# Linear-attention products in quarters of the array, two units at a time, in a kernel that ends in a SiLU network

## The chip, the cores and the metric

The kernel runs on one core of a Trainium2 chip. Its metric is the device time of one execution in microseconds, taken as the median of several runs. TensorE is written PE below, VectorE DVE, ScalarE ACT, GpSimd POOL and the engine that issues most transfers SP.

## The reference

The inputs are r, k and v of shape 4 x 8 x 768 x 48 (batch, heads, time, head dimension), decays w and bonuses u of 8 x 48, and the two weight matrices of a network, 384 x 2048 and 2048 x 384. The first part walks through time with a 48 x 48 state per batch and head:

```
for t in range(S):
    cur = einsum('bhd,bhe->bhde', u * k[t], v[t])
    y[t] = einsum('bhd,bhde->bhe', r[t], state + cur)
    state = w * state + einsum('bhd,bhe->bhde', k[t], v[t])
```

The second part takes y as 3072 tokens of 384 values, multiplies by w_in, applies h * sigmoid(h), and multiplies by w_out. The result is 3072 x 384 in float32.

## The kernel before, in words

Time is cut into 6 chunks of 128 steps (C = 128, HC = 64 is half of it). A **unit** is one chunk of one batch: 24 units, numbered so that unit i is batch i % 4 of chunk i // 4. Four units make up one chunk, which is called a stage here (units 4 to 7, 8 to 11 and so on); its 512 tokens go through the network together.

In a unit the recurrence becomes matrix products. `turn` transposes r and k with PE (16 fp32 transposes of 64 rows, two row halves of the array) into a PSUM tile `t`; `decay` multiplies them by powers of w on DVE, giving `rT` and `kT`. `product` (L202) multiplies kT with rT for each of 8 heads, keys on partitions and queries along the free axis, in fp32, with contraction 48: heads in partitions 0 to 47 and 64 to 111 use the upper and the lower rows of the array. `masked` zeroes the pairs whose key is not earlier than the query. `outputs` (L216) adds state times r (L223) and masked product times v (L228) in the PSUM tile `ys`, and forms the state's increment from keys and values (L235). `evict_y` (L245) adds the bonus term and writes `y16`; `state` updates the state; `turn_y` (L274) transposes y16 into `xT`, by PE and a copy on ACT for units 0 to 5, by a DMA transpose on SP for units 6 to 23.

The network is `l1` (three fp16 matmuls of 512 columns and a SiLU on ACT for each of 16 column blocks; it reads `xT` of all four units of the stage) and `l2` (four fp16 matmuls of 384 columns; four such parts make one output tile, which is copied and stored). These calls are **fillers** in one first-in first-out list; `fill(n)` emits the next n of them, or fewer where the list is empty. In stages from the second on, 32 fillers come in with each finished stage (16 of l1, 16 of l2) and 8 are emitted per unit.

The order of instructions on each engine is the order of the Python text: nothing reorders it. The work of units 0 to 3 is written out by hand with part of the first stage's l1. Then a loop over single units follows; each iteration calls, in order: product(i), the POOL work of unit i+1, masked(i), fill(2), turn(i+1), decay(i+1), outputs(i), evict_y(i), turn_y(i), state(i), load(i+4), casts of i+1, fill(6), and after the last unit of a stage the list gets the fillers of that stage. When the loop starts the list holds 24 fillers: 8 of l1 (each two column blocks of half the stage) and 16 of l2.

[...]Tiles tagged `att` (t, a, ys) take two banks each and have two buffers; tiles tagged `moe` (l1's hps, l2's ops, yT) take one bank each and have four.

Of the kernel before, what the change touches and what calls it, by code (L numbers as in the profile page):

```python
# [8 lines left out]
FP = mybir.dt.float32  # L9
F16 = mybir.dt.float16  # L10
# [5 lines left out]
def kernel(  # L16
# [14 lines left out]
    C = 128  # L31
# [18 lines left out]
    def unit(i):  # L50
        return divmod(i, B)

    wpT = cst.tile([PR, NP], FP)
    w_bc = cst.tile([128, HD], FP)
    u_bc = cst.tile([128, H, D], FP)
    rin = [big.tile([128, H, 64], FP, name=f"rin{i}") for i in range(NIN)]
    kin = [big.tile([128, H, 64], FP, name=f"kin{i}") for i in range(NIN)]
    vin = [big.tile([128, H, D], FP, name=f"vin{i}") for i in range(NIN)]
    kc = [big.tile([128, H, 64], F16, name=f"kc{i}") for i in range(2)]
    st = [big.tile([PR, NP, PW], FP, name=f"st{b}") for b in range(B)]  # L60
    st16 = [big.tile([PR, NP, PW], F16, name=f"stb{b}") for b in range(B)]
    win = big.tile([128, NQ, DFF], F16)
# [8 lines left out]
    def load(i):  # L71
        if i >= NU:
            return
        ld(i, rin, r)
        ld(i, kin, k)
        ld(i, vin, v)
# [21 lines left out]
    for i in range(NIN):  # L98
# [12 lines left out]
    nc.gpsimd.affine_select(  # L111
        out=maskM, in_=maskM, compare_op=ALU.is_ge, fill=0.0,
        base=-1, channel_multiplier=-1, pattern=[[1, C]])
    ident16 = cst.tile([128, 128], F16)
    nc.gpsimd.tensor_copy(out=ident16, in_=ident)
    for b in range(B):
# [3 lines left out]
    for i in range(NIN):  # L120
        nc.vector.memset(rin[i][:, :, D:64], 0.0)
        nc.vector.memset(kin[i][:, :, D:64], 0.0)
    for i in range(2):
        nc.vector.memset(kc[i][:, :, D:64], 0.0)

    lnwT = cst.tile([PR, NP], FP)
# [22 lines left out]
    def L(i):  # L149
        return live.setdefault(i, {})  # L150

    def bonus_products(i):
        n = i % NIN
        ku = wrk.tile([128, H, D], FP, name="ku")
        nc.gpsimd.tensor_tensor(out=ku, in0=kin[n][:, :, 0:D], in1=u_bc, op=ALU.mult)  # L155
        L(i)["rku_f"] = wrk.tile([128, H, D], FP, name="rku_f")
        nc.gpsimd.tensor_tensor(out=L(i)["rku_f"], in0=rin[n][:, :, 0:D], in1=ku, op=ALU.mult)  # L157

    def decayed_k(i):
        eng = nc.vector if i < B else nc.gpsimd  # L160
        eng.tensor_tensor(out=kc[i % 2][:, :, 0:D], in0=kin[i % NIN][:, :, 0:D],  # L161
                                in1=lamC, op=ALU.mult)

    def bonus_sum(i):
        L(i)["rku"] = wrk.tile([128, H], FP, name="rku")
        nc.vector.tensor_reduce(out=L(i)["rku"], in_=L(i)["rku_f"],  # L166
                                axis=mybir.AxisListType.X, op=ALU.add)

    def bonus_v(i):
# [2 lines left out]
                                in1=L(i)["rku"].unsqueeze(2).broadcast_to([128, H, D]),  # L172
                                op=ALU.mult)

    def cast_v(i):
        L(i)["v16"] = wrk.tile([128, H, D], F16, name="v16", bufs=3)
        nc.scalar.copy(out=L(i)["v16"], in_=vin[i % NIN])

    def turn(i):
        n = i % NIN  # L180
        t = L(i)["t"] = ps.tile([128, 2, 2, NP, HC], FP, name="t", tag="att", bufs=2)
        for x, src in enumerate((rin, kin)):
            flat = src[n].rearrange("p h d -> p (h d)")
            for p in range(NP):
                for y in range(2):
                    rows = slice(HC * y, HC * y + HC)
                    nc.tensor.transpose(t[0:PR, y, x, p, :], flat[rows, 128 * p:128 * p + PR],  # L187
                                        ident[rows, rows])

    def decay(i):  # L190
        for x, key, lam in ((0, "rT", lamR), (1, "kT", lamK)):
            L(i)[key] = wrk.tile([PR, NP, C], FP, name=key)
            nc.vector.tensor_tensor(  # L193
                out=L(i)[key].rearrange("p g (y t) -> p y g t", y=2),
                in0=L(i)["t"][0:PR, :, x], in1=lam.rearrange("p g (y t) -> p y g t", y=2),
                op=ALU.mult)

    def cast_r(i):
        L(i)["rT16"] = wrk.tile([PR, NP, C], F16, name="rT16")
        nc.scalar.copy(out=L(i)["rT16"], in_=L(i)["rT"])  # L200

    def product(i):  # L202
        a = L(i)["a"] = ps.tile([128, 2, NP, C], FP, name="a", tag="att", bufs=2)
        rT, kT = L(i)["rT"], L(i)["kT"]
        for p in range(NP):
            for j, r0 in ((0, 0), (1, 64)):
                nc.tensor.matmul(a[:, j, p, :], kT[r0:r0 + D, p, :], rT[r0:r0 + D, p, :],  # L207
                                 start=True, stop=True)

    def masked(i):  # L210
        am = L(i)["am"] = wrk.tile([128, 2, NP, C], F16, name="am")
        nc.vector.tensor_tensor(  # L212
            out=am.rearrange("p h g c -> p (h g) c"), in0=L(i)["a"].rearrange("p h g c -> p (h g) c"),
            in1=maskM.unsqueeze(1).broadcast_to([128, H, C]), op=ALU.mult)

    def outputs(i):  # L216
        sc, b = unit(i)
        v16 = L(i)["v16"]
        ys = L(i)["ys"] = ps.tile([128, 2, 512], FP, name="ys", tag="att", bufs=2)
        y = ys[:, 0, 0:HD].rearrange("p (h d) -> p h d", h=H)  # L220
        for p in range(NP):
            if sc:
                nc.tensor.matmul(y[:, 2 * p:2 * p + 2, :],  # L223
                                 L(i)["rT16"][0:PR, p, :],
                                 st16[b][:, p, :], start=True, stop=False)
            for j in range(2):
                h = 2 * p + j
                nc.tensor.matmul(y[:, h, :], L(i)["am"][:, j, p, :], v16[:, h, :],  # L228
                                 start=not sc, stop=(not sc or j == 1))
        if sc < NCH - 1:  # L230
            sps = ys[:, 1, 0:HD].rearrange("p (g n) -> p g n", g=NP)
            kf = kc[i % 2].rearrange("p h d -> p (h d)")
            vf = v16.rearrange("p h d -> p (h d)")
            for p in range(NP):
                nc.tensor.matmul(sps[:, p, :], kf[:, 128 * p:128 * p + 128],  # L235
                                 vf[:, PW * p:PW * p + PW], start=True, stop=True)
# [6 lines left out]
                                    in1=wCT.unsqueeze(2).broadcast_to([PR, NP, PW]), op=ALU.mult)  # L243

    def evict_y(i):  # L245
        y = L(i)["ys"][:, 0, 0:HD].rearrange("p (h d) -> p h d", h=H)
        L(i)["y16"] = wrk.tile([128, H, D], F16, name="y16")
        nc.vector.tensor_tensor(out=L(i)["y16"], in0=y, in1=L(i)["vu"], op=ALU.add)  # L248

    def state(i):  # L250
        sc, b = unit(i)
        if sc == NCH - 1:
            return
        sps = L(i)["ys"][:, 1, 0:HD].rearrange("p (g n) -> p g n", g=NP)
        for p0, c0 in ((0, 0), (64, D)):
            dst = st[b][p0:p0 + D, :, c0:c0 + D]
            src = sps[p0:p0 + D, :, c0:c0 + D]
            if sc:
                nc.vector.tensor_tensor(out=dst, in0=src,  # L259
                                        in1=L(i)["sdec"][p0:p0 + D, :, c0:c0 + D], op=ALU.add)  # L260
            else:
                nc.scalar.copy(out=st16[b][p0:p0 + D, :, c0:c0 + D], in_=src)
                nc.scalar.copy(out=dst, in_=src)
        if sc:
            nc.gpsimd.tensor_copy(out=st16[b], in_=st[b])  # L265
# [22 lines left out]
    def l1(sc, b0, nb, ft):  # L288
        if sc not in gts:
            gts[sc] = wrk.tile([128, NFT, B * C], F16, name="gT", bufs=2)  # L290
        m = B // nb
        hps = ps.tile([128, m, nb * C], FP, name="hps", tag="moe", bufs=4)
        for f in range(m):
            for q in range(NQ):
                nc.tensor.matmul(hps[:, f, :], win[:, q, (ft + f) * 128:(ft + f + 1) * 128],  # L295
                                 xts[sc][:, q, b0:b0 + nb, :].rearrange("p b t -> p (b t)"),
                                 start=(q == 0), stop=(q == NQ - 1))
        nc.scalar.activation(out=gts[sc][:, ft:ft + m, b0 * C:(b0 + nb) * C], in_=hps, func=AF.Silu)  # L298
# [21 lines left out]
    def fill(n):  # L320
        for _ in range(n):
            if fillers:
                fillers.pop(0)()
# [87 lines left out]
    bonus_sum(4)  # L411
    bonus_v(4)
    decayed_state(4)
    fillers.extend([lambda ft=ft: l1(0, 2, 2, ft) for ft in range(0, NFT, 2)])
    fillers.extend(second(0))

    for i in range(B, NU):
        sc, b = unit(i)
        product(i)
        if i + 1 < NU:  # L420
            bonus_products(i + 1)
            decayed_k(i + 1)
        masked(i)
        fill(2)
        if i + 1 < NU:
            turn(i + 1)
            decay(i + 1)
        outputs(i)
        evict_y(i)
        turn_y(i, i < 6)  # L430
        state(i)
        load(i + NIN)
        if i + 1 < NU:
            cast_v(i + 1)
            cast_r(i + 1)
            bonus_sum(i + 1)
            bonus_v(i + 1)
            decayed_state(i + 1)
        fill(6)
        if b == B - 1:  # L440
            fillers.extend(first(sc) + second(sc))
    fill(len(fillers))


# [28 lines left out]
```

## Time and profile before

| what | value |
|---|---|
| median of 3 runs | 214.6 us (214.12 to 215.39) |
| the profiled execution | 214.33 us, of which the span is 212.6 us |
| PE busy | 192.9 us, 91% of the span |
| DVE, ACT, POOL busy | 103.0, 99.0, 118.1 us |
| l1 matmuls (L295) | 68.2 us busy, 336 records |
| l2 matmuls (L307) | 65.9 us busy, 384 records |
| products (L207) | 30.6 us busy, 384 records for 192 instructions |
| transposes of r and k (L187) | 11.6 and 10.6 us busy, 192 records each |
| DMA transposes of y16 (L279) | 18, 2.3 us in the median from issue to landing |

The span runs from the first to the last instruction of the profile. "Busy" is time in which at least one instruction of the group is in flight. Matmuls overlap, so that a mean duration (304 ns for a record of L207) is longer than the step from one record to the next. A line of the timeline gives start, length and kind of a run of like instructions, and in brackets the idle time ahead of it and what ended it.

### The profile page before, as it was taken

The page shows a single profiled execution, that of the slowest core. Times are in us where ns is not written, and L with a number is a line of the kernel's source. Part 1 is how long each engine was busy: PE and PEld are TensorE (multiplying, and loading weights), DVE is VectorE, ACT ScalarE, POOL GpSimd, SP SyncE. Part 2 cuts the span into 40 slices and gives each one's busy share as a digit, 9 for nine tenths or more (in the row PEclk, how much of TensorE's full clock was granted, in tenths as well). Part 3 has the DMA queues.
Part 4 walks back from the last instruction along what each step waited for, and adds up shares of the span by engine and source line. Part 5 has one row for each costly group of instructions (what it writes and reads, how often), then busy time and mean ns, then how long its engine had stood idle before and what let it go on. Part 6 is the DMA issues. An engine that isn't in the chain of part 4 may idle for free.

```text
span 212.6 us, 4734 instructions
## 1 busy us (share of the span) xinstructions
PE 192.9 (91%) x1858; PEld 122.7 (58%) x1858; DVE 103.0 (48%) x173; ACT 99.0 (47%) x190; POOL 118.1 (56%) x151
## 2 busy tenths in 40 slices
PE   1677898798986999999999999999999999999993
PEld 0566587665663655675556666556665556654551
DVE  3677386543656545563573474565456246300121
ACT  2403868633321767233864324783226782159400
POOL 8677549966296567558558557756854662000000
PEclk9999999999998899999999999999999999999999
DMA  6899999999175255277346267525627010220011
GB/s 113 177 180 212 206 203 172 195 159 211 40 167 130 58 113 102 52 185 156 93 87 130 59 167 189 100 48 114 138 89 187 19 22 18 78 94 0 0 74 74
DMA packets 90262, 24.49 MB, mean 115 GB/s; under 512 B 83328, under 2 KB 90240, under 8 KB 90240
## 3 DMA queue, kind: packets, MB, share of 16 engines
q1 hardware_dynamic: 85824, 20.65, 44.6%
q0 software_dynamic: 3712, 3.15, 9.6%
q10 hardware_dynamic: 704, 0.40, 0.9%
q8 instruction: 14, 0.23, 0.4%
q14 instruction: 8, 0.07, 0.1%
HBM read 20.84 MB, written 4.72 MB: 120 GB/s over the span
## 4 chain that ended last, share of the span: by engine, by line
PE 86%; DVE 5%; DMA 3%; issue 2%; POOL 1%; ACT 0%; ACTq 0%; DVEq 0%; POOLq 0%
PE hps L295 31%; PE ops L307 30%; PE a L207 12%; PE t L187 7%; DMA u_bc<-in_u_dram 2%; PE ys L223 2%; PE ys L228 2%; DVE rT L193 2%; PE ys L235 1%; DMA xT<-y 1%; DVE y L248 1%; PE yT L283 1%; DVE am L212 1%; DVE kT L193 1%; DVE kc L161 1%
## 5 line engine op out<-in xcount | busy, mean ns | idle before, releaser
L295 PE MATMUL hps<-xT,win 128*128 128x512 f16 (+1 forms) x336 | 68.2, 357 | 2.1 <-DMA xT<-y 1.6
L307 PE MATMUL ops<-wout,gT 128*128 128x384 f16 x384 | 65.9, 326 | 0.0
L298 ACT ACTIVATE gT<-hps 128x512 f16<-128x512 f32 x96 | 56.1, 597 | 17.7 <-PE hps L295 14.5
L212 DVE TENSOR_TENSOR am<-a,maskM 128x1024 f16<-128x1024 f32 x24 | 29.4, 1224 | 56.1 <-PE a L207 56.0
L307 PEld LDWEIGHTS <-gT 128*128 128x128 f16 x384 | 36.2, 98 | 23.6
L295 PEld LDWEIGHTS <-win 128*128 128x128 f16 x336 | 32.3, 100 | 29.7 <-issue 2.5
L207 PE MATMUL a<-rT,kT 48*128 48x128 f32 x384 | 30.6, 304 | 3.4 <-DVE kT L193 3.4
L207 PEld LDWEIGHTS a<-rT,kT 48*128 48x128 f32 x384 | 25.8, 204 | 10.8 <-issue 6.5
L265 POOL CAST stb<-st 112x384 f16<-112x384 f32 x16 | 8.1, 505 | 39.1 <-DVE st L259 26.2
L171 POOL TENSOR_TENSOR vu<-vin,rku 128x384 f32<-128x384 f32 x24 | 19.9, 830 | 17.5 <-DVE rku L166 17.1
L193 DVE TENSOR_TENSOR rT<-t,lamR 112x512 f32<-112x512 f32 x24 | 16.5, 689 | 20.6 <-PE t L187 14.7
L200 ACT CAST rT<-rT 112x512 f16<-112x512 f32 x20 | 12.4, 618 | 29.2 <-DVE rT L193 29.2
L155 POOL TENSOR_TENSOR ku<-kin,u_bc 128x384 f32<-128x384 f32 x24 | 24.1, 1003 | 3.0 <-DMA u_bc<-in_u_dram 1.8
L157 POOL TENSOR_TENSOR rku_f<-rin,ku 128x384 f32<-128x384 f32 x24 | 24.6, 1025 | 1.9
L312 ACT COPY osb<-ops 128x384 f32<-128x384 f32 x20 | 9.6, 480 | 29.3 <-PE ops L307 29.3
L161 POOL TENSOR_TENSOR kc<-kin,lamC 128x384 f16<-128x384 f32 x20 | 20.0, 1001 | 0.0
L193 DVE TENSOR_TENSOR kT<-t,lamK 112x512 f32<-112x512 f32 x24 | 16.3, 680 | 0.0
L187 PE MATMUL t<-ident,rin 64*112 64x64 f32 x192 | 11.6, 247 | 5.1 <-DMA rin<-in_r_dram 4.2
L187 PEld LDWEIGHTS t<-ident,rin 64*112 64x112 f32 x192 | 8.2, 145 | 13.1 <-DVE am L212 4.6
L166 DVE TENSOR_REDUCE rku<-rku_f 128x8 f32<-128x384 f32 x24 | 13.2, 550 | 2.3 <-POOL rku_f L157 1.7
L248 DVE TENSOR_TENSOR y<-ys,vu 128x384 f16<-128x384 f32 x24 | 13.2, 548 | 1.8 <-PE ys L235 1.1
L242 POOL TENSOR_TENSOR sdec<-st,wCT 112x384 f32<-112x384 f32 x16 | 13.2, 828 | 0.0
(46 smaller groups left out, 132.2 us busy)
## 6 DMA issues: line engine op xcount, KB each, us to landing
rin<-in_r_dram SPq DMA_DIRECT2D x24, 192.0 KB, 3.0
kin<-in_k_dram SPq DMA_DIRECT2D x24, 192.0 KB, 3.5
vin<-in_v_dram SPq DMA_DIRECT2D x24, 192.0 KB, 3.6
out_dram<-osb SPq DMA_DIRECT2D x24, 192.0 KB, 2.5
win<-in_moe_w_in_dram POOLq DMA_DIRECT2D x4, 384.0 KB, 6.1
wout<-in_moe_w_out_dram POOLq DMA_DIRECT2D x4, 384.0 KB, 8.6
xT<-y SPq DMA_TRANSPOSE x18, 2.3
u_bc<-in_u_dram ACTq DMA_DIRECT2D x1, 192.0 KB, 5.0
```

The lines of the kernel that those rows point to most:

```text
L155: nc.gpsimd.tensor_tensor(out=ku, in0=kin[n][:, :, 0:D], in1=u_bc, op=ALU.mult)
L157: nc.gpsimd.tensor_tensor(out=L(i)["rku_f"], in0=rin[n][:, :, 0:D], in1=ku, op=ALU.mult)
L161: eng.tensor_tensor(out=kc[i % 2][:, :, 0:D], in0=kin[i % NIN][:, :, 0:D], in1=lamC, op=ALU.mult)
L171: nc.gpsimd.tensor_tensor(out=L(i)["vu"], in0=vin[i % NIN], in1=L(i)["rku"].unsqueeze(2).broadcast_to([128, H, D]), op=ALU.mult)
L187: nc.tensor.transpose(t[0:PR, y, x, p, :], flat[rows, 128 * p:128 * p + PR], ident[rows, rows])
L193: nc.vector.tensor_tensor(out=L(i)[key].rearrange("p g (y t) -> p y g t", y=2), in0=L(i)["t"][0:PR, :, x], in1=lam.rearrange("p g (y t) -> ...
L207: nc.tensor.matmul(a[:, j, p, :], kT[r0:r0 + D, p, :], rT[r0:r0 + D, p, :], start=True, stop=True)
L212: nc.vector.tensor_tensor(out=am.rearrange("p h g c -> p (h g) c"), in0=L(i)["a"].rearrange("p h g c -> p (h g) c"), in1=maskM.unsqueeze(1 ...
L248: nc.vector.tensor_tensor(out=L(i)["y16"], in0=y, in1=L(i)["vu"], op=ALU.add)
L295: nc.tensor.matmul(hps[:, f, :], win[:, q, (ft + f) * 128:(ft + f + 1) * 128], xts[sc][:, q, b0:b0 + nb, :].rearrange("p b t -> p (b t)"), ...
L298: nc.scalar.activation(out=gts[sc][:, ft:ft + m, b0 * C:(b0 + nb) * C], in_=hps, func=AF.Silu)
L307: nc.tensor.matmul(ops, gts[sc][:, ft, b * C:(b + 1) * C], wout[:, ft, :], start=(ft == 0), stop=(ft == NFT - 1))
```

## The change

The loop over single units becomes a loop over pairs (i, i+1) for units 4 to 23.

- `product_pair` takes the place of `product` there. Each head's product is cut by key halves: early keys (64) with all 128 queries, late keys (64) with the late 64 queries; late keys with early queries are not computed. The even unit writes early keys to partitions 0 to 63 and late keys to 64 to 127, the odd unit the other way round ("crossed"), so that four consecutive instructions (two units, two heads) address four different 64 x 64 quarters of the array.
- `masked` uses a mask with swapped halves for the odd unit, and `outputs` uses a copy of v with swapped halves (`vx`, two ACT copies).
- All fp32 work of a pair stands in two blocks: the products, and the transposes of both units of the next pair.
- The att tiles become two fixed tiles that take turns. For units from 4 on, the outputs go to two `moe` tiles, `yp` and `sp`, in place of `ys`. kc has four buffers, v16 four.
- turn(5), decay(5) and the casts of unit 5, and four of the eight l1 fillers, move ahead of the loop. The list holds 20 fillers when the loop starts. A pair emits 4, 2, 2, 2, 2 and 4 fillers. The stage's new fillers are appended right after the outputs of its last unit.

```diff
+    def product_pair(i):
+        a = [next_att().rearrange("p j (g c) -> p j g c", g=NP) for _ in range(2)]
...
+        for s0, c0 in ((0, 0), (HC, HC)):
+            for p in range(NP):
+                for e in range(2):
+                    rT, kT = L(i + e)["rT"], L(i + e)["kT"]
+                    o0 = s0 if e == 0 else HC - s0
+                    for j, r0 in ((0, 0), (1, 64)):
+                        nc.tensor.matmul(a[e][o0:o0 + HC, j, p, c0:C],
+                                         kT[r0:r0 + D, p, s0:s0 + HC],
+                                         rT[r0:r0 + D, p, c0:C],
+                                         start=True, stop=True)
...
-        ys = L(i)["ys"] = ps.tile([128, 2, 512], FP, name="ys", tag="att", bufs=2)
+        if sc:
+            yp = ps.tile([128, 512], FP, name="yp", tag="moe", bufs=4)
+            L(i)["y"] = yp[:, 0:HD]
...
+            if sc:
+                sp = ps.tile([128, 512], FP, name="sp", tag="moe", bufs=4)
...
-    fillers.extend([lambda ft=ft: l1(0, 2, 2, ft) for ft in range(0, NFT, 2)])
+    bonus_products(5)
+    decayed_k(5)
+    l1(0, 2, 2, 0)
+    turn(5)
+    decay(5)
+    cast_v(5)
+    for ft in (2, 4, 6):
+        l1(0, 2, 2, ft)
...
+    fillers.extend([lambda ft=ft: l1(0, 2, 2, ft) for ft in range(8, NFT, 2)])
     fillers.extend(second(0))
-    for i in range(B, NU):
+    for i in range(B, NU, 2):
...
+        product_pair(i)
+        for n in nxt:
+            bonus_products(n)
+            decayed_k(n)
         masked(i)
+        masked(i + 1)
+        fill(4)
         outputs(i)
         evict_y(i)
         turn_y(i, i < 6)
         state(i)
+        fill(2)
+        outputs(i + 1)
+        evict_y(i + 1)
+        turn_y(i + 1, i < 6)
+        state(i + 1)
+        if b:
+            fillers.extend(first(sc) + second(sc))
+        fill(2)
+        for n in nxt:
+            turn(n)
+            decay(n)
         load(i + NIN)
+        load(i + 1 + NIN)
...
+        for n in nxt:
+            fill(2)
+            cast_r(n)
+        fill(4)
```

More of the change, by code (lines that the diff above doesn't have):

```diff
@@ L51, in unit, with next_att @@
         return divmod(i, B)
+    att = [ps.tile([128, 2, 512], FP, name=f"att{i}") for i in range(2)]
+    turns = []
+    def next_att():
+        turns.append(0)
+        return att[len(turns) % 2]
     wpT = cst.tile([PR, NP], FP)
@@ L58 @@
     vin = [big.tile([128, H, D], FP, name=f"vin{i}") for i in range(NIN)]
-    kc = [big.tile([128, H, 64], F16, name=f"kc{i}") for i in range(2)]
+    kc = [big.tile([128, H, 64], F16, name=f"kc{i}") for i in range(NIN)]
     st = [big.tile([PR, NP, PW], FP, name=f"st{b}") for b in range(B)]
@@ L113 @@
         base=-1, channel_multiplier=-1, pattern=[[1, C]])
+    maskX = cst.tile([128, C], FP)
+    nc.scalar.copy(out=maskX[0:HC, :], in_=maskM[HC:C, :])
+    nc.scalar.copy(out=maskX[HC:C, :], in_=maskM[0:HC, :])
     ident16 = cst.tile([128, 128], F16)
@@ L122 @@
         nc.vector.memset(kin[i][:, :, D:64], 0.0)
-    for i in range(2):
+    for i in range(NIN):
         nc.vector.memset(kc[i][:, :, D:64], 0.0)
@@ L160, in decayed_k @@
         eng = nc.vector if i < B else nc.gpsimd
-        eng.tensor_tensor(out=kc[i % 2][:, :, 0:D], in0=kin[i % NIN][:, :, 0:D],
+        eng.tensor_tensor(out=kc[i % NIN][:, :, 0:D], in0=kin[i % NIN][:, :, 0:D],
                                 in1=lamC, op=ALU.mult)
@@ L173, in bonus_v, with crossed @@
                                 op=ALU.mult)
+    def crossed(i):
+        return i >= B and i % 2 == 1
     def cast_v(i):
-        L(i)["v16"] = wrk.tile([128, H, D], F16, name="v16", bufs=3)
-        nc.scalar.copy(out=L(i)["v16"], in_=vin[i % NIN])
+        v16 = L(i)["v16"] = L(i)["vy"] = wrk.tile([128, H, D], F16, name="v16", bufs=4)
+        nc.scalar.copy(out=v16, in_=vin[i % NIN])
+        if crossed(i):
+            vx = L(i)["vy"] = wrk.tile([128, H, D], F16, name="vx", bufs=2)
+            nc.scalar.copy(out=vx[0:HC], in_=v16[HC:C])
+            nc.scalar.copy(out=vx[HC:C], in_=v16[0:HC])
     def turn(i):
         n = i % NIN
-        t = L(i)["t"] = ps.tile([128, 2, 2, NP, HC], FP, name="t", tag="att", bufs=2)
+        t = L(i)["t"] = next_att().rearrange("p y (x g t) -> p y x g t", x=2, g=NP)
         for x, src in enumerate((rin, kin)):
@@ L202, in product @@
     def product(i):
-        a = L(i)["a"] = ps.tile([128, 2, NP, C], FP, name="a", tag="att", bufs=2)
+        a = L(i)["a"] = next_att().rearrange("p j (g c) -> p j g c", g=NP)
         rT, kT = L(i)["rT"], L(i)["kT"]
@@ L208, in product @@
                                  start=True, stop=True)
+    def product_pair(i):
+        a = [next_att().rearrange("p j (g c) -> p j g c", g=NP) for _ in range(2)]
+        for e in range(2):
+            L(i + e)["a"] = a[e]
+        for s0, c0 in ((0, 0), (HC, HC)):
+            for p in range(NP):
+                for e in range(2):
+                    rT, kT = L(i + e)["rT"], L(i + e)["kT"]
[5 more added lines that the diff above has]
+                                         start=True, stop=True)
     def masked(i):
@@ L213, in masked @@
             out=am.rearrange("p h g c -> p (h g) c"), in0=L(i)["a"].rearrange("p h g c -> p (h g) c"),
-            in1=maskM.unsqueeze(1).broadcast_to([128, H, C]), op=ALU.mult)
+            in1=(maskX if crossed(i) else maskM).unsqueeze(1).broadcast_to([128, H, C]), op=ALU.mult)
     def outputs(i):
         sc, b = unit(i)
-        v16 = L(i)["v16"]
-        ys = L(i)["ys"] = ps.tile([128, 2, 512], FP, name="ys", tag="att", bufs=2)
-        y = ys[:, 0, 0:HD].rearrange("p (h d) -> p h d", h=H)
+        v16, vy = L(i)["v16"], L(i)["vy"]
+        if sc:
+            yp = ps.tile([128, 512], FP, name="yp", tag="moe", bufs=4)
+            L(i)["y"] = yp[:, 0:HD]
+        else:
+            ys = next_att()
+            L(i)["y"], L(i)["sps"] = ys[:, 0, 0:HD], ys[:, 1, 0:HD]
+        y = L(i)["y"].rearrange("p (h d) -> p h d", h=H)
         for p in range(NP):
@@ L227, in outputs @@
                 h = 2 * p + j
-                nc.tensor.matmul(y[:, h, :], L(i)["am"][:, j, p, :], v16[:, h, :],
+                nc.tensor.matmul(y[:, h, :], L(i)["am"][:, j, p, :], vy[:, h, :],
                                  start=not sc, stop=(not sc or j == 1))
         if sc < NCH - 1:
-            sps = ys[:, 1, 0:HD].rearrange("p (g n) -> p g n", g=NP)
-            kf = kc[i % 2].rearrange("p h d -> p (h d)")
+            if sc:
+                sp = ps.tile([128, 512], FP, name="sp", tag="moe", bufs=4)
+                L(i)["sps"] = sp[:, 0:HD]
+            sps = L(i)["sps"].rearrange("p (g n) -> p g n", g=NP)
+            kf = kc[i % NIN].rearrange("p h d -> p (h d)")
             vf = v16.rearrange("p h d -> p (h d)")
@@ L245, in evict_y @@
     def evict_y(i):
-        y = L(i)["ys"][:, 0, 0:HD].rearrange("p (h d) -> p h d", h=H)
+        y = L(i)["y"].rearrange("p (h d) -> p h d", h=H)
         L(i)["y16"] = wrk.tile([128, H, D], F16, name="y16")
@@ L253, in state @@
             return
-        sps = L(i)["ys"][:, 1, 0:HD].rearrange("p (g n) -> p g n", g=NP)
+        sps = L(i)["sps"].rearrange("p (g n) -> p g n", g=NP)
         for p0, c0 in ((0, 0), (64, D)):
@@ L413 @@
     decayed_state(4)
-    fillers.extend([lambda ft=ft: l1(0, 2, 2, ft) for ft in range(0, NFT, 2)])
+    bonus_products(5)
[6 more added lines that the diff above has]
+        l1(0, 2, 2, ft)
+    cast_r(5)
+    bonus_sum(5)
+    bonus_v(5)
+    decayed_state(5)
+    fillers.extend([lambda ft=ft: l1(0, 2, 2, ft) for ft in range(8, NFT, 2)])
     fillers.extend(second(0))
-    for i in range(B, NU):
+    for i in range(B, NU, 2):
         sc, b = unit(i)
[L419 to L422, printed above, removed]
+        nxt = range(i + 2, min(i + 4, NU))
+        product_pair(i)
+        for n in nxt:
+            bonus_products(n)
+            decayed_k(n)
         masked(i)
[L424 to L427, printed above, removed]
+        masked(i + 1)
+        fill(4)
         outputs(i)
@@ L431 @@
         state(i)
-        load(i + NIN)
[L433 to L441, printed above, removed]
+        fill(2)
[9 more added lines that the diff above has]
+            decay(n)
+        load(i + NIN)
+        load(i + 1 + NIN)
+        for n in nxt:
+            bonus_sum(n)
+            cast_v(n)
+            bonus_v(n)
+            decayed_state(n)
+        for n in nxt:
+            fill(2)
+            cast_r(n)
+        fill(4)
     fill(len(fillers))
```

## The prediction

> **What bounds the kernel now.** I read the busy shares first, then the slices, the timeline of a middle stage, the chain and the windows around its one break.
>
> ```profile
> PE 192.9 (91%) x1858; PEld 122.7 (58%) x1858; DVE 103.0 (48%) x173; ACT 99.0 (47%) x190; POOL 118.1 (56%) x151
> ...
> PE   1677898798986999999999999999999999999993
> ...
> PEclk9999999999998899999999999999999999999999
> ```
>
> From the 14th slice to the last but one PE never rests, and no other engine is near full. So from unit 8 on, the time is the sum of PE's own work, and what another engine does counts only where PE starts to wait for it. PE's timeline from the end of unit 9 shows what a unit costs:
>
> ```profile
> 90.30 1.16 PE L207 MATMUL a<-rT,kT 48*128 48x128 f32 x16
> 91.40 1.47 PE L307 MATMUL ops<-wout,gT 128*128 128x384 f16 x8
> 92.80 0.44 PE L187 MATMUL t<-ident,rin 64*112 64x64 f32 x8
> 93.08 0.39 PE L187 MATMUL t<-ident,kin 64*112 64x64 f32 x8
> 93.40 0.22 PE L223 MATMUL ys<-stb,rT 112*128 112x96 f16 x1
> ```
>
> Start to start, a product takes 1.09 us and a unit's transposes 0.59; outputs run from 93.40 to 93.96, 0.56. A part of l2 is 4 x 0.1625 = 0.65 us, a part of l1 the same. In the trace's single records the 16 of a product start in 8 couples, 6.6 ns apart within a couple (the two row halves at once); the couples step by 0.1115 us, but the first step is 0.21 and the last couple holds PE 0.21. With the 0.09 that pass between the preceding filler's last column and the first record, a product is 8 x 0.1115 + 0.295 fixed = 1.19 us. The transposes (64 columns) step by 0.056: 8 x 0.056 + 0.24 fixed = 0.69.
>
> The one break after the start-up is the end of the second stage, unit 7, where the list of fillers is empty:
>
> ```profile
> 64.06 0.55 DVE y L248
> ...
> 64.64 2.33 DMA xT<-y
> ...
> 67.00 2.09 PE hps L295 x6
> ```
>
> This is the chain: y is evicted, the DMA transpose lands, and only then can l1 start. PE idles 0.87 (for the mask), 0.58 (for kT) and 1.55 us there. Then PE is slow:
>
> ```profile
> 64.28:67.69 3.41, 1.85 (x20) 1.40 (x21) 2.72 (x5) 0.00 (x0) 2.29 (x4) 1.00 0.31 67
> 67.69:71.10 3.41, 3.41 (x37) 2.17 (x36) 0.86 (x2) 1.73 (x4) 2.75 (x3) 0.50 0.76 150
> ```
>
> The first figure after the length is PE's busy time, the third last the granted clock. A window of 3.41 us with 1.85 busy (1.56 idle) is followed by one at half clock. The same instructions took 8.03 us from 67.00 to the product at 75.03 and 6.54 from 99.04 to 105.58: 1.5 us lost.
>
> [...]
>
> **The change, part by part** (gains negative).
>
> *Products.* A pair has 32 instructions, 64 records: half with 128 query columns, half with 64. If four quarters run at once, that is 8 steps of 0.1115 and 8 of 0.056 (the transposes' step, also 64 columns) plus 0.295 = 1.64 us against 2 x 1.19 = 2.37: -0.74 per pair, -7.4 for ten. [...]If column halves don't overlap at all, every step doubles: 8 x 0.223 + 8 x 0.112 + 0.295 = 2.98, +6.1. No row shows which. I take 1.75, near the first, [...]: **-6.2**.
>
> *Transposes.* Nine pairs have both units' transposes in one block, which saves 0.24 each: **-2.2**. Their records are the same.
>
> *Unit 4 and 5.* PE waits 1.20 and 1.25 us for y16 ahead of its own transposes, since decay (two of 0.68) stands before evict_y on DVE. That is now behind it; the rest, 0.2 until DVE starts and 0.55, stays: **-0.9**.
>
> *Ahead of the loop.* l1 now follows turn_y(3) at once; product(4), 1.1 us, used to cover the ACT copy of xT. The same order at unit 1 shows a wait of 0.57: **+0.6**. Bounds: 0 and 1.
>
> *The end of a stage.* The loop starts with 20 fillers, not 24, and a pair emits 16. Pair (4,5) leaves 4; pair (6,7) takes them in its fill(4) and has none left. After its outputs 32 come in, 10 go, 22 stay; pair (8,9) leaves 6; of pair (10,11), fill(4) and the fill(2) between the outputs take exactly these 6. So after outputs(11) the next thing in PE's order is l1 of the stage that unit 11 has just finished, and behind it the transposes of 12 and 13, which can't pass it. Every stage repeats this. Before, fill(6) and a product, 3.9 + 1.2 us, stood between. What PE waits for, from the start of the outputs, is best read at unit 23, where DVE is free:
>
> ```profile
> 184.50 0.56 DVE L248 TENSOR_TENSOR y<-ys,vu 128x384 f16<-128x384 f32 x1 [0.66 <-PE ys L228]
> ...
> 185.09 1.58 SPq L279 DMA_TRANSPOSE xT<-y  x1
> ...
> DMA to landing us min/median/max: 2.3/2.3/4.0
> ```
>
> The outputs began at 183.82. Eviction starts 0.68 later, the transpose is issued at 1.27 (1.3 with the store of the last l2 tile, which is ahead of it in SP's queue: copy done at 0.6, issue 0.65), lands at 3.6, and PE starts at 3.65. Of this outputs fill 0.56: 3.1 us idle at units 11, 15 and 19. At unit 7 no filler separates the two outputs, so evict_y(6) and state(6) (0.55 + 0.71) delay DVE: 3.75. At unit 23 outputs are shorter (0.42) and this landing took 2.7: 3.55. Sum 16.6, less the 3.0 at unit 7 now: **+13.6**. Bounds per end 2.8 and 4.
>
> *The clock.* 3.1 us of idle over a grid of 3.41 us leaves at least 1.55 in one window, what was enough above. Half clock for one window costs up to 1.7; where the boundary falls early its first part is idle anyway. I take 1.4 each, 7.0, less today's 1.5: **+5.5**. Bounds: +1 (two of five) and +7.
>
> *Costed at nothing.* vx, two ACT copies of half the partitions per pair (0.3 to 0.5 us each by the 0.31 and 0.51 us rows of L262 and L177): ACT has 16 x 0.60 for SiLU, 2 x 0.51 and 2 x 0.62 for casts and 0.9 for vx, 12.8 us, in a 15 us pair of l1, and none waits on vx before the next pair. Mask and kc set-up sit under ACT's and DVE's waits of 2.3 and 2.5 us for the first loads. masked of both units, 2.45 us on DVE, lies under fill(4), 2.6: were a filler missing there, PE would wait about 0.5. yp and sp take half of the moe buffers; each reuse comes two fillers (1.3 us) or more after its release at about 0.7 (yp) and 1.4 us (sp, which is written 0.4 later). POOL needs 10.4 us per pair. Loads are issued later, but a pair ahead of use, against 3.5 us to landing.
>
> The sum is 13.6 + 5.5 + 0.6 - 6.2 - 2.2 - 0.9 = +10.4, on the profiled execution's 214.3 (span 212.6 and 1.7 around it): 224.7; the median stands 0.3 higher, so **225.0 us**.
>
> **Rivals.** *(1) Column halves of the array don't overlap.* For it: no such row exists. [...]The product term turns from -6.2 to +6.1: 237. *(2) Stage ends stay cheap, and the change is faster or equal.* The gains are 6.2 + 2.2 + 0.9 - 0.6 = 8.7, and 4.5 are lost at unit 7 today; the kernel gains only where a stage end costs under 13.2 / 5 = 2.6 us, idle and clock together. Idle of 2.8 with the full clock throughout, and products at 1.64, give 213.9 + 0.3 = 214.2, no change. For it: gaps of 1.2 us at units 4 and 5 left the clock alone. Against it: no transpose of 18 landed under 2.3 us, and 54% busy was too little. *(3) Weights in the same rows go one after the other:* [...]counted with the forecast.
>
> **How the numbers follow.** A measurement of this kernel tells about 0.5% from no change. Forecast with (3): 0.85; rival (1): 0.10; rival (2): 0.05, most of it split between no change and a gain. The range reaches from the cheap ends (2.9 idle, clock +2.5, products at 1.64: 220) to (3) with dear ends (231), 219 to 231; rival (1) is left out.
>
> **What would show it.** PE should wait for DMA xT<-y five times, 3 to 4 us each, about 16.6 in all, with half-clock windows after them; product_pair should hold PE some 1.65 us start to start; the waits for the mask at the loop should be gone; DVE should evict y within 0.3 us of its matmul. Waits for xT under 8 us in all would make the prediction wrong, and so would a product of 2.5 us or more.

## The result, and the profile after

The changed kernel takes **224.05 us** in the median (222.67 to 225.56, 4 runs) against 214.44 for the kernel before, measured with it: ratio **1.044**, 95% interval 1.036 to 1.053, slower. The forecast was 225.0, range 219 to 231. The profiled execution took 223.16 us, its span is 221.5, so 8.9 us more than before.

The busy shares, the slices and the granted clock of the changed kernel:

```profile
PE 187.8 (85%) x2178; PEld 119.9 (54%) x2178; DVE 101.7 (46%) x175; ACT 106.5 (48%) x212; POOL 117.4 (53%) x151
...
PE   2566897989939999949999949999949999679993
...
PEclk9999999999996999999999988999999999979998
```

PE is busy 5.1 us less although the span is 8.9 longer. Its row, full from the 14th slice before, now has a hole of one slice (5.5 us) in five places: at slices 12, 18, 24, 30 and across 35 and 36. Behind three of them (12, 24 and 35/36) the clock dips as well; the dip in the last slice lies behind the last matmul. The chain of waits names the holes:

```profile
PE 72%; issue 7%; DVE 6%; DMA 5%; POOL 5%; ACT 2%; SPq 1%; ACTq 0%; POOLq 0%; DVEq 0%
```

PE had 86% of the chain before. PE's waits (engine and line, what it waited for, sum, times, longest):

```profile
PE hps L335 <- DMA xT<-y: 10.5, 3, 3.8
PE hps L335 <- issue: 6.4, 2, 3.2
```

Both lines are one thing: five waits of l1 for xT, 16.9 us. For two of them the transpose had landed 0.2 us before l1 started, and the profile puts them down to "issue". That is read from the timeline of all engines at the end of the third stage, units 10 and 11:

```profile
94.76 0.21 PE L260 MATMUL yp<-stb,rT 112*128 112x96 f16 x1
...
95.15 0.33 PE L275 MATMUL sp<-v,kc 128*128 128x96 f16 x4
98.60 1.46 PE L335 MATMUL hps<-xT,win 128*128 128x512 f16 x6 [3.12 <-issue]
```

```profile
95.40 0.56 DVE L288 TENSOR_TENSOR y<-yp,vu 128x384 f16<-128x384 f32 x1 [0.67 <-issue]
...
95.51 0.43 SPq L356 DMA_DIRECT2D out_dram<-osb  x1
...
96.04 1.18 SPq L319 DMA_TRANSPOSE xT<-y  x1
```

outputs(11) starts at 94.76; eviction starts 0.64 later, the transpose is issued at 1.28 behind the store, and l1 starts at 3.84 (forecast: 0.68, 1.3 and 3.65). The gain is in the same timeline, in the block of products of a pair:

```profile
88.80 1.57 PE L237 MATMUL att<-rT,kT 48*64 48x128 f32 x64
90.30 2.77 PE L347 MATMUL ops<-wout,gT 128*128 128x384 f16 x16
```

64 records take 1.50 us from their start to that of the next block, 1.59 with the 0.09 us that pass before the first one starts. Two single products took 2.37 with theirs.

### The profile page after: what moved, and what is told of

The parts are those of the page before. It is cut to its first block, busy times and chain, and to the rows that moved or that the text cites. A ratio compares the mean times of both kernels' runs of the same rounds, so it can differ in the third digit from the quotient of the medians.

```text
span 221.5 us, 5379 instructions
## 1 busy us (share of the span) xinstructions
PE 187.8 (85%) x2178; PEld 119.9 (54%) x2178; DVE 101.7 (46%) x175; ACT 106.5 (48%) x212; POOL 117.4 (53%) x151
## 4 chain that ended last, share of the span: by engine, by line
PE 72%; issue 7%; DVE 6%; DMA 5%; POOL 5%; ACT 2%; SPq 1%; ACTq 0%; POOLq 0%; DVEq 0%
PE hps L335 31%; PE ops L347 23%; PE att L237 6%; PE att L204 6%; DMA xT<-y 3%; PE att L224 2%; DMA u_bc<-in_u_dram 2%; DVE st L299 2%; DVE y L288 1%; POOL rku_f L167 1%; POOL ku L165 1%; PE yp L265 1%; PE yp L260 1%; PE yT L323 1%; ACT xT L324 1%
## 5 line engine op out<-in xcount | busy, mean ns | idle before, releaser
L335 PE MATMUL hps<-xT,win 128*128 128x512 f16 (+1 forms) x336 | 71.5, 368 | 18.0 <-DMA xT<-y 10.5
L244 DVE TENSOR_TENSOR am<-att,maskM 128x1024 f16<-128x1024 f32 x14 | 17.1, 1223 | 37.9 <-PE att L237 35.4
L210 DVE TENSOR_TENSOR rT<-att,lamR 112x512 f32<-112x512 f32 x24 | 16.5, 686 | 30.3 <-PE att L204 15.0
L288 DVE TENSOR_TENSOR y<-yp,vu 128x384 f16<-128x384 f32 x20 | 11.1, 557 | 15.7 <-PE yp L265 5.1
L204 PE MATMUL att<-ident,rin 64*112 64x64 f32 x192 | 12.0, 255 | 5.8 <-DMA rin<-in_r_dram 4.0
L210 DVE TENSOR_TENSOR kT<-att,lamK 112x512 f32<-112x512 f32 x24 | 16.3, 679 | 0.0
L237 PEld LDWEIGHTS att<-rT,kT 48*64 48x64 f32 x640 | 14.3, 133 | 3.5 <-issue 3.5
L237 PE MATMUL att<-rT,kT 48*64 48x64 f32 (+1 forms) x640 | 15.7, 247 | 0.0
L204 PEld LDWEIGHTS att<-ident,rin 64*112 64x112 f32 x192 | 8.8, 155 | 11.1 <-issue 4.5
L244 DVE TENSOR_TENSOR am<-att,maskX 128x1024 f16<-128x1024 f32 x10 | 12.1, 1214 | 0.0
```

What stands on the lines that cost most here:

```text
L210: nc.vector.tensor_tensor(out=L(i)[key].rearrange("p g (y t) -> p y g t", y=2), in0=L(i)["t"][0:PR, :, x], in1=lam.rearrange("p g (y t) -> ...
L237: nc.tensor.matmul(a[e][o0:o0 + HC, j, p, c0:C], kT[r0:r0 + D, p, s0:s0 + HC], rT[r0:r0 + D, p, c0:C], start=True, stop=True)
L244: nc.vector.tensor_tensor(out=am.rearrange("p h g c -> p (h g) c"), in0=L(i)["a"].rearrange("p h g c -> p (h g) c"), in1=(maskX if crossed ...
```

## The experiments

**The wait itself: six fillers held back.**

```diff
-        fill(2)
+        fill(0 if i == 6 else 2)
...
-        fill(4)
+        fill(0 if i == 6 else 4)
```

> The changed kernel with six fillers of the pair (6,7) held back, so that six l2 parts of the stage before stand between the outputs of units 11, 15, 19 and 23 and the first l1 that needs their xT. All other parts of the change stay: yp and sp in the moe buffers, vx, the later POOL work. Theory (l1 is placed right behind the outputs it depends on): the four waits of 3.1 to 3.4 us at units 11, 15, 19 and 23 go, 13.1 us, and the half-clock windows behind them, 1.5 us each where they fell (about 3); the wait at unit 7 stays, shortened by the 1.0 us of the transposes that now come first. 223.2 - 13.1 - 3 - 1 = 206, within 205 to 209. Rival (the buffers of yp and sp, or the casts and POOL work of a pair, keep PE waiting, whatever stands behind the outputs): new waits of 1 us or more per pair appear in their place, and the time stays above 214.

Measured: 205.81 us (205.38 to 206.97), ratio to the kernel before 0.959 (0.955 to 0.962), faster. PE's waits and the slices of its profile:

```profile
PE hps L335 <- DMA xT<-y: 3.8, 2, 3.6
```

```profile
PE   1666898898992999999999999999999999999993
...
PEclk9999999999998899999999999999999999999999
```

Of the five holes one is left, at unit 7, and with the four others 18 us are gone. No new wait came: yp and sp still share the moe buffers, vx is still copied, POOL still works on two units in a row. So the place of l1 behind its own outputs was the cause of the loss, and from unit 8 on nothing else in the pair loop costs PE a wait of more than 0.2 us. The wait at unit 7 shrank by 0.2 only, not 1.0: the transposes of r and k did go first, but the DMA transposes of units 6 and 7 held SP's queue for 3.42 us in place of 2.58, so that xT landed that much later. The shift from a loss of 4.4% to a gain of 4.1% is a matter of where six calls stand.

**The wait put into the kernel before.** The opposite test: all else as before, but in the last unit of a stage the fillers stand ahead of the outputs.

```diff
-        fill(2)
+        fill(8 if b == B - 1 else 2)
...
-        fill(6)
+        if b < B - 1:
+            fill(6)
```

> The kernel before with one thing moved: in the last unit of each stage the eight fillers all stand ahead of the outputs, none behind, so that after the outputs only the next unit's product stands ahead of the l1 that needs their xT. Products, buffers and the single-unit loop are those of before. Theory (the place of l1 alone costs the time): PE waits for kT and then for xT at units 11, 15 and 19 as it does at unit 7 today, 0.6 and 1.6 us each, and some 3.4 us at unit 23, where no product follows: 10 us of new waits in all, and half-clock windows after most of them (1.5 us each): 224 to 231. Rival (only the pair loop's order makes the wait matter): no more than 216.

Measured: 233.08 us (230.96 to 234.96), ratio 1.081 (1.075 to 1.088). The place alone costs 17.5 us here (215.55 for the kernel before, measured with it), about as much as in the changed kernel (224.05 less 205.81, 18.2). PE's waits for xT and kT grew by 10.5 us in the profile (15.5 against 5.0), as expected. But the time lies 2 us above the expected 224 to 231: half-clock windows came behind every stage end, and at units 7, 19 and 23 for two windows, where one had been allowed for. The granted clock was 0.948 to 0.963 in five of the six runs and 0.939 in the profiled one, against 0.98 to 1.00 for the kernel before.

**What the quarters save.** Two kernels on top of e1_hold6, one with row halves in one block, one with quarters that leave nothing out.

```diff
-        product_pair(i)
+        product(i)
+        product(i + 1)
...
-        return i >= B and i % 2 == 1
+        return False
```

> e1_hold6 with the products of both units written as before (128 keys by 128 queries, two row halves of the array), one after the other in one block; the odd unit isn't crossed and has no vx. Theory (the quarters save because the late keys with early queries are left out): 16 steps of 0.1115 and 0.295 fixed are 2.08 us per pair against 1.59 in the changed kernel: slower than e1_hold6 by 0.49 x 10 = 4.9 us. Rival (the saving of a pair came from having one fp32 block in place of two, and the quarters bring nothing): no slower than e1_hold6, within 1 us.

```diff
-        for s0, c0 in ((0, 0), (HC, HC)):
+        for s0, c0 in ((0, 0), (HC, 0)):
```

> e1_hold6 with the late keys multiplied with all 128 queries in the quarters as well, so that nothing is left out; the mask zeroes the extra part. Theory (four quarters run at once and only what is left out saves): 16 steps of 0.1115 and 0.295 fixed, 2.08 us per pair, slower than e1_hold6 by 4.9 us and equal to e2_rows within 1 us. Rival (the quarters themselves are quicker than row halves, for the shorter weight loads): within 2 us of e1_hold6. Rival (column halves don't run at once): slower than e2_rows by 15 us or more.

Measured: e2_rows 208.25 us (207.21 to 210.26), ratio 0.971 (0.965 to 0.976); e3_full_quarters 209.56 (206.81 to 210.43), ratio 0.973 (0.968 to 0.978). The blocks in PE's timeline, first e2_rows, then e3_full_quarters, each with the l2 part that follows:

```profile
84.54 2.06 PE L224 MATMUL att<-rT,kT 48*128 48x128 f32 x32
86.53 0.66 PE L347 MATMUL ops<-wout,gT 128*128 128x384 f16 x3
```

```profile
86.20 1.98 PE L237 MATMUL att<-rT,kT 48*64 48x128 f32 x64
88.11 0.66 PE L347 MATMUL ops<-wout,gT 128*128 128x384 f16 x3
```

A pair's products take 1.99 us in row halves, 1.91 in full quarters with twice the records, and 1.50 in quarters with the late keys cut. So four quarters do run at once: 64 records with 128 query columns take no longer than the 32 in row halves. But quarters alone bring only 0.08, although a weight load of PEld lasts 133 ns in the mean with 64 columns (L237 of the changed kernel) and 204 with 128 (L207 of the kernel before). Of the 0.78 between 2.37 and 1.59, one block in place of two brings 0.29, the quarters 0.08, and the work left out, in quarters, 0.41. By the block, e2_rows should be 4.9 us behind e1_hold6. The profiles, each with one half-clock window, are 3.8 apart (207.5 and 203.7); e2_rows makes up 0.86 by a shorter wait at unit 7 (2.73 against 3.59), because there the two DMA transposes held SP's queue for 2.57 us, not 3.42. The medians are only 2.4 apart, because three of six runs of e2_rows kept the full clock (207.2 to 207.3) and no run of e1_hold6 did. e3_full_quarters ended 1.3 above e2_rows, a little more than the 1 us expected, although its blocks are shorter: only one of its six runs kept the full clock. The rivals fall: one block for both units isn't all, quarters that leave nothing out are 3.8 us slower than e1_hold6, and column halves do overlap (1.91 us against 1.99).

**The clock: useless matmuls in the wait.**

```diff
             fillers.extend(first(sc) + second(sc))
+            idle = ps.tile([128, 512], FP, name="idle", tag="moe", bufs=4)
+            for _ in range(12):
+                nc.tensor.matmul(idle, win[:, 0, 0:128], win[:, 1, 0:512], start=True, stop=True)
```

> The changed kernel with 12 matmuls of 512 columns that nobody uses (2.6 us) right behind the outputs of the last unit of each stage, where PE waits for xT; they don't wait for anything. The waits for xT end when they did. Theory (the half-clock windows follow from PE's rest): no half-clock window after the start-up, time shorter by 1.5 us for each that fell, 219 to 221. Rival (the clock falls for another reason, the fp32 blocks for one): the half-clock windows stay, 223 to 225.

Measured: 219.68 us (218.96 to 222.87), ratio 1.022 (1.019 to 1.026). Five of the six runs had a granted clock of 0.999 or 1.000, where the changed kernel had 0.959 to 0.974. So 2.6 us of added PE work at each stage end makes the kernel 4.4 us quicker: in these runs the half-clock windows follow from PE's rest, and cost about that much in the median run. The profiled execution was the longest of the six (222.87): it still has one half-clock window, behind unit 7, and its waits for xT didn't end when they did before but up to 1.2 us later, again with SP's queue held longer by DMA transposes (3.77 us for those of units 6 and 7, against 2.58).

**A version that beats both.** The pair (4,5) emits 10 fillers, so that six are left behind unit 7 as well; turn(5) comes ahead of the first l1.

```diff
-    l1(0, 2, 2, 0)
     turn(5)
     decay(5)
+    l1(0, 2, 2, 0)
...
-        fill(2)
+        fill({4: 1, 6: 0}.get(i, 2))
         outputs(i + 1)
...
-        fill(2)
+        fill(1 if i == 4 else 2)
...
-            fill(2)
+            fill(1 if i == 4 else 2)
             cast_r(n)
-        fill(4)
+        fill(2 if i == 4 else 4)
```

> A version meant to beat both: the changed kernel where the pair (4,5) emits 10 fillers in place of 16, so that six l2 parts stand behind the outputs of unit 7 too (and, as in e1_hold6, behind those of 11, 15, 19 and 23); turn(5) and decay(5) stand ahead of the first l1 of the second half. Theory (waits of PE are all that is left to gain): the wait at unit 7, 3.6 us in e1_hold6, goes to under 0.5, the half-clock window behind it (1.5 us) goes, 0.5 us of the wait for xT of unit 3 goes, and up to 0.8 us comes in as product_pair(6) waits for kT: 200 to 203. Rival (fewer fillers in pair (4,5) only move the wait to the masks and to kT): no better than e1_hold6, 205 to 206.

Measured: **199.80 us** (199.10 to 201.28), ratio **0.928** (0.923 to 0.933) to the kernel before. Its slices:

```profile
PE   2546799897999999999999999999999999999992
```

That is just under the expected 200 to 203. No wait for xT by l1 through the DMA is left, the longest wait of PE from unit 6 on is 0.17 us, and the clock stays at 0.997 to 1.000. From the 11th slice to the last but one PE doesn't rest.

## Why the prediction was right, step by step

It forecast +10.4 us for the profiled execution; +8.8 came (223.16 against 214.33). The mechanism, l1 right behind its own outputs at every stage end, was the one that the runs show. That the sum came so close is partly luck, as the terms below tell.

- **End of a stage**, forecast +13.6: the waits are 3.79, 3.12, 3.33, 3.25 and 3.39 us, 16.9, less the 3.0 at unit 7 before: **+13.9**. The count of fillers (20 at the start, exactly none left at each stage end) was the step that decided, and e1_hold6, which changes only that, turns the result round. At unit 23 the landing was no slower than elsewhere, so 3.39 in place of 3.55.
- **Clock**, forecast +5.5: three half-clock windows in the profiled execution, about 1.5 each (from one stage's first l1 to the next, without the idle: 30.2 us with a window, 28.6 without), less 1.5 before: **+3.1**. This term was mis-sized. The step that failed is "at least 1.55 in one window, what was enough above": windows with up to 2.0 us of rest were followed by the full clock (last section). The three other runs of the changed kernel had clocks of 0.959 to 0.967 against the profiled 0.974, by my estimate one or two windows more (a window of 3.41 us at half clock takes 0.008 off the mean over a span of 221.5 us); two of them took 1.8 and 2.4 us longer than the profiled one, the third 0.5 less.
- **Products**, forecast -6.2: ten times 2.37 - 1.59 is **-7.8**, a little more than the best case (1.64). In the single records of the block shown above, the four of a group start within 0.02 us, and the groups step by 0.109 us with 128 query columns and by 0.058 with 64, so both step sizes were right (0.1115 and 0.056); the fixed part is 0.26 in place of 0.295. The 1.75 was my estimate, with no view of before that shows column halves; its allowance above the best case wasn't needed.
- **Transposes**, forecast -2.2: a block of two units takes 1.04 + 0.09 against 2 x 0.69: **-2.2**.
- **Units 4 and 5**, forecast -0.9: waits of 0.48 and 0.55 against 1.20 and 1.25: **-1.4**. The work that I put behind them as staying, 0.75, was 0.5.
- **Ahead of the loop**, forecast +0.6: **+0.57**, at 36.16 of the changed kernel.
- **Start-up**, not in the sum: PE reaches the transposes of unit 3's y at 35.82, before at 34.14: **+1.7**. At unit 2, PE now waits 1.53 us for ACT's copies of unit 0's state, 0.88 for the mask before: the two fixed att tiles give turn(2) the tile that held the outputs of unit 0. And the trace's records of the clock begin, at full speed, at 28.9 us, before at 26.7; the 8 transposes of k took 0.64 us at 26.45 and 0.39 at 32.91, so by my estimate the 2.2 us more at the slow pace cost some 1 us. No run shows that the change did this.

These make +7.9; 1.0 us of the 8.9 in the span isn't assigned. The clock, the products and units 4 and 5 came out 4.5 us below the forecast together; the start-up and the unassigned rest, neither of them foreseen, gave 2.7 back. The lower end of the range has a slip in its sum: its own terms (2.9 idle, clock +2.5, products at 1.64) give 218.7, not 220. The upper end, 231, counts in a cost of rival (3), which was not shown by a trace. Of what I costed at nothing, e1_hold6 shows it from the eighth unit on: neither vx, nor the masks under fill(4), nor the shared moe buffers, nor POOL made PE wait.

Rival (1), column halves that don't overlap, is out by e3_full_quarters (1.91 us for 64 records); rival (2), cheap stage ends, by the five holes; rival (3), weights one after the other, by the 1.50 us of a block, and by the weight loads in it: in the same single records the four of a group start within 0.02 us and last 0.13 each.

## What to carry to other kernels

In a list of independent work that hides latency, count what is left at each point where a dependent item follows its own producer; the average amount of cover is the same in the slow kernel and in the fast one (eight calls per unit in a middle stage). A saving of 1.0 us per pair on the engine that bounds was real, some 10 us in all, and one list that ran out at every stage end cost 17; holding six items back kept the gain and removed most of the loss. And here a rest of PE cost more than its length, so that even useless matmuls in it paid (219.68 us against 224.05).

## What the runs showed of the hardware

**Busy time alone does not tell what clock follows.** In the changed kernel, stretches at half clock begin at 66.40, 131.25, 196.11 and 220.00 us, 19, 19 and 7 times 3.41 us apart. The windows below are of 3.41 us on that grid: PE busy first, granted clock third last. The first two and the next three are of the changed kernel, the last three of e5_before_late, where the window behind 204.95 is at half clock too.

```profile
62.99:66.40 3.41, 1.11 (x6) 0.52 (x6) 0.30 (x1) 0.26 (x1) 0.72 (x2) 1.00 0.54 108
66.40:69.81 3.41, 3.41 (x37) 2.19 (x36) 1.70 (x3) 2.76 (x6) 0.00 (x0) 0.50 1.10 216
158.55:161.96 3.41, 2.19 (x34) 1.53 (x30) 2.35 (x6) 0.48 (x1) 2.52 (x4) 1.00 0.34 100
161.96:165.38 3.42, 1.39 (x7) 0.52 (x8) 0.00 (x0) 0.55 (x1) 0.51 (x1) 1.00 0.72 158
165.38:168.79 3.41, 3.41 (x44) 2.05 (x44) 2.64 (x5) 3.29 (x8) 0.00 (x0) 1.00 1.09 215
```

```profile
133.27:136.68 3.41, 1.58 (x29) 1.27 (x24) 3.33 (x7) 0.76 (x2) 0.99 (x2) 1.00 0.30 89
136.68:140.09 3.41, 2.79 (x8) 0.86 (x10) 0.69 (x1) 0.61 (x2) 3.33 (x5) 0.50 0.82 162
...
201.53:204.95 3.42, 1.42 (x19) 0.92 (x17) 0.56 (x1) 0.48 (x1) 0.00 (x0) 1.00 0.30 106
```

A window with 1.11 us of fp16 matmuls was followed by half clock; one with 1.39 us, all of it l1, by the full clock. But one with 1.58 us, most of it one fp32 product of 48 rows (1.16), was followed by half clock too, and so was one with 1.85 (54% of it) in the kernel before, with such a product in it, and one with 1.42 us of fp16 matmuls, of which the last 0.5 are the narrow ones of the outputs. What sorts these windows no run here tests; it stays open. Nor is it the length of one rest: after waits of 3.12 and 3.25 us (units 11 and 19) the clock of the changed kernel stayed full, and after one of 1.55 us at unit 7 the kernel before was at half clock.

**Quarters in fp32.** In the block of the changed kernel at 88.80, four quarters of the array at once, 48 rows each, took 64 records in 1.50 us, 23 ns for each, and the four of a group start within 0.02 us; with nothing left out they are 4% quicker than row halves (1.91 against 1.99).
